# Random tie-breaking, with one seed, in the list scheduler of a fused attention and channel-mix kernel

## The chip, the cores and the metric

The kernel runs on one core of a Trainium2 chip. The metric is the device time of one execution in microseconds (us). It holds the whole computation, from the inputs in HBM to the output in HBM. The core's engines are named as the profile names them: PE (TensorE, matmuls) with PEld (its weight loads), DVE (VectorE), ACT (ScalarE), POOL (GpSimd) and SP (SyncE, which here only issues DMAs).

## The reference

Softmax attention with RMS-normalised queries and keys over batch 8, 12 heads, 448 tokens, head size 64. Its output, as 768 features per token, goes through a channel mix: each token is blended with the one before it by two learned vectors, multiplied by `w_k` (768 x 1024), clipped at zero and squared, multiplied by `w_v` (1024 x 768), and gated by the sigmoid of a second blend times `w_r` (768 x 768). Everything is float32 at the surface; the three weight matrices come in float64.

```python
q_n, k_n = rmsnorm(q, g_q), rmsnorm(k, g_k)
scores = scale * np.matmul(q_n, k_n.transpose(0, 1, 3, 2))
attn = np.exp(scores - np.max(scores, axis=-1, keepdims=True))
attn = attn / (np.sum(attn, axis=-1, keepdims=True) + 1e-09)
attn_out = np.matmul(attn, v)
...
xk = mu_k * x + (1.0 - mu_k) * x_prev
xr = mu_r * x + (1.0 - mu_r) * x_prev
k = np.maximum(xk @ w_k, 0.0)
v = k * k @ w_v
r = 1.0 / (1.0 + np.exp(-(xr @ w_r)))
return (r * v).astype(np.float32)
```

## The kernel before

**Tiling.** The work on the attention side goes by quads of heads (24 of them, `quads`) and pairs (48, `pairs`). A quad has seven score groups, each a tile of 128 rows by 448 keys for two heads. Most products are formed from two 16-bit parts of each operand, high and low, so that a product is three matmuls; the first three quads (`U32 = 3`) use 32-bit matmuls instead. After each pair's attention, two blends of the token with its predecessor are made (`mix`), and when the six pairs of a batch are there, the MoE part of the batch follows: eight 448-wide products with `w_k` (`moe`, `square`), then for each block of 128 tokens and each half of the features a product with `w_r` and one with `w_v` (`gate`, `store`). The weights are decoded from float64 and split into 16-bit parts in the course of the first quarter of the run (`wload`, `weights`, `wsplit`).

**Who does what.** PE does all matmuls and, for the early groups, transposes. DVE finds the row maxima of scores (`expo`), forms low parts (`split`), blends, decodes weights and multiplies by the gate. ACT does exponentials, high parts, casts and activations. POOL does scalings and differences in SBUF. SP issues the loads of q, k and v, the DMA transposes of probabilities and of q and k, and the stores; ACT issues the weight loads.

**Buffers.** PSUM has eight banks in one ring, of which scores may hold five (`SC_SHARE`), the MoE products and the weight decoding two (`MM_SHARE`), and attention outputs and weight statistics two (`OT_SHARE`). There are three q/k buffers, two V buffers, four tiles for probabilities (`NAT_BUFS`, one more later).

**What sets the order.** The order of instructions on each engine is not written out; a planner, `Plan`, makes it while the program is built. Every piece of work (`load`, `stats`, `preps`, `expo`, `split`, `weights`, `moe` and so on) is a Python generator, called a thread, that yields one operation after another, or a condition to wait for. The planner keeps one clock per engine, in nanoseconds, from a price list (`price` for DVE, ACT and POOL; the matmuls' price stands in their `form`; DMAs are priced in `emit`). `advance` fetches a thread's next operation and works out when its operands are ready by the planner's own account. `run` then takes, over and over, the operation with the smallest key:

```python
k = max(self.clk[th[2][0].eng] + wait, th[3] + slack) - PS * (th[1]() if callable(th[1]) else th[1])
if best is None or k < key:
    best, key = th, k
```

Here `th[3]` is the readiness, `th[1]` the thread's priority and `PS` is 0.1, so that a hundred points of priority are worth 10 ns. `slack` holds matmuls of attention back (`MARGIN` 600, `MARGIN_A` 400, `MARGIN_V` 1200), `wait` charges a switch of the PE tile mode (`SWITCH` 600) and one kind of ACT sequence (`ACC_GAP` 130). The comparison is strict, so of equal keys the one whose thread stands first in the list of threads wins: the thread that was spawned earlier. Priorities that matter for ties are `PRIO_E` 400 (`expo`, `probs`, `setup`, `load`), `PRIO_M` 400 (`square`, `gate`, `store`), `PRIO_R` 320, `PRIO_V` 310, `PRIO_O` 300, `PRIO_P` 200 (`split`), `PRIO_S` 150 (`scores`), `PRIO_Q` and `PRIO_A` 50 (`stats`, `preps`, `attends`), 0 (`mixk`, `moe`), and for the weights one formula that all their threads share (`wprio`). `pick` chooses ACT or DVE for some copies out of PSUM (in `turn` and `probs_pe`, for the first three quads) by whose clock is behind.

The planner prices TensorE at one speed throughout. All instructions are recorded by one helper line, so the profile shows L273 for nearly all of them; they are told apart by their tiles. `ps` is a PSUM bank, `sums` the maxima and sums of a score group, `nat` a tile of probabilities or of prepared q and k, `stk` transposed q and k, `pT` transposed probabilities, `wf` a decoded weight block, `raw` its float64 words, `kk` the squared activations, `xk` and `xr` the two blends. In the first stretch, buffers of `kk` and `xk` are lent out for other tiles (`KK_LENT`, `XK_LENT`), so that these two names then also stand for raw weights, loaded q and k, or probabilities.

Of the kernel before, what the change touches and what calls it, by code (L numbers as in the profile page):

```python
# [1 line left out]

# [52 lines left out]
PS = 0.1  # L55
# [75 lines left out]
class Op:  # L131
    def __init__(self, eng, fn, kw, form=None):
        self.eng, self.fn, self.kw, self.form = eng, fn, kw, form
        outs = [kw[k] for k in ("out", "accum_out") if kw.get(k) is not None]
        self.reads = [span(x) for k, x in kw.items() if k not in ("out", "accum_out") and hasattr(x, "tensor")]
        self.writes = [span(x) for x in outs if hasattr(x, "tensor")]
        self.reads = [y for x in self.reads for y in x]
        self.writes = [y for x in self.writes for y in x]
# [64 lines left out]
        return lambda form=None, **kw: Op(self.name, f, {k: aps(x) if hasattr(x, "shape") else x for k, x in kw.items()}, form)  # L203


class Plan:
    LAT = 35

    def __init__(self, tc):
        self.tc = tc  # L210
        self.clk = dict.fromkeys(("PE", "DVE", "ACT", "POOL", "SP"), 0.0)
        self.last, self.use, self.threads = {}, {}, []
        self.form, self.dma_free, self.acc, self.n = None, {"SP": 0.0, "ACT": 0.0}, False, 0
        self.held = {"DVE": [], "POOL": []}

    def margin(self, form):
        if form == "moe":
            return 0
        if form == "av" and self.st["want"] != "xk":
            return MARGIN_A  # L220
        return MARGIN_V if form == "v" else MARGIN
# [5 lines left out]
        return min(self.clk["ACT"], self.clk["DVE"])  # L227

    def spawn(self, gen, prio=0):
        th = [gen, prio, None, 0.0]  # L230
        self.threads.append(th)
        self.advance(th)

# [13 lines left out]
    def advance(self, th):  # L247
        try:
            x = next(th[0])
        except StopIteration:  # L250
            self.threads.remove(th)
            return
        if isinstance(x, Op):
            x = [x]
        th[2] = x
        th[3] = self.ready(x) if isinstance(x, list) else 0.0

    def note(self, op, fin):
# [66 lines left out]
    def run(self):  # L325
        while self.threads:
            best, key = None, None
            for th in list(self.threads):
                if not isinstance(th[2], list):
                    if not th[2]():  # L330
                        continue
                    self.advance(th)
                    if th not in self.threads or not isinstance(th[2], list):
                        continue
                slack = self.margin(th[2][0].form[0]) if th[2][0].eng == "PE" else 0
                mode = MODE.get(th[2][0].form[0], 0) if th[2][0].eng == "PE" else None
                wait = SWITCH if mode == 0 and self.form else 0
                if self.acc and th[2][0].eng == "ACT" and th[2][0].kw.get("accum_out") is not None:
                    wait += ACC_GAP
                k = max(self.clk[th[2][0].eng] + wait, th[3] + slack) - PS * (th[1]() if callable(th[1]) else th[1])  # L340
                if best is None or k < key:
                    best, key = th, k
            if best is None:
                if any(isinstance(th[2], list) or th[2]() for th in self.threads):
                    continue
                assert not self.threads, [(th[0].__name__, th[2]) for th in self.threads]
                break
            r = self.ready(best[2])
            if r > best[3] + 1:
                best[3] = r  # L350
                continue
            self.emit(best[2])
            self.advance(best)
# [884 lines left out]
```

## Time and profile before

| | |
|---|---|
| median of 3 runs | 1015.41 us (1015.3 to 1017.15) |
| the profiled execution's own time | 1015.21 us |
| its span, first to last instruction | 1013.4 us |
| PE busy | 926.0 us, 91% of the span |
| DVE busy | 812.7 us, 80% |
| ACT busy | 746.0 us, 74% |
| POOL busy | 691.8 us, 68% |
| mean granted TensorE clock | 0.961 |
| bytes moved | 148.17 MB, 146 GB/s |

The busy times are of the whole span; the engines do different work early and late, so the stretches have to be read one by one. A busy PE is not a PE at its peak, since its matmuls overlap. A row of waits gives the engine and tile that stood idle, the engine and tile that ended the idle time, the total, the number of waits and the longest. A timeline row gives the start, the length, the engine, and the operation with output and inputs; in brackets stand the idle time of the engine ahead of it and what ended it.

### The profile page before, as it was taken

The page shows a single profiled execution, that of the slowest core. Times are in us where ns is not written, and L with a number is a line of the kernel's source. Part 1 is how long each engine was busy: PE and PEld are TensorE (multiplying, and loading weights), DVE is VectorE, ACT ScalarE, POOL GpSimd, SP SyncE. Part 2 cuts the span into 40 slices and gives each one's busy share as a digit, 9 for nine tenths or more (in the row PEclk, how much of TensorE's full clock was granted, in tenths as well). Part 3 has the DMA queues.
Part 4 walks back from the last instruction along what each step waited for, and adds up shares of the span by engine and source line. Part 5 has one row for each costly group of instructions (what it writes and reads, how often), then busy time and mean ns, then how long its engine had stood idle before and what let it go on. Part 6 is the DMA issues. An engine that isn't in the chain of part 4 may idle for free. (4 is left out here: it accounts for less than half of the span.)

```text
span 1013.4 us, 18593 instructions
## 1 busy us (share of the span) xinstructions
PE 926.0 (91%) x6082; PEld 485.8 (48%) x6082; DVE 812.7 (80%) x2260; ACT 746.0 (74%) x1756; POOL 691.8 (68%) x734
## 2 busy tenths in 40 slices
PE   2588869669999999999999999899999999999998
PEld 2354434335544555455545555355545454455564
DVE  5879998999998698979997998799997989763000
ACT  3667878878788789888887887878886988952311
POOL 2787889743798747877886859855987478556501
PEclk9878979869999999999999999999999999999999
DMA  7322349667788789569847977869858884640000
GB/s 248 119 80 86 118 120 221 170 166 169 172 165 168 143 197 203 133 152 201 207 105 173 214 158 161 161 131 201 175 126 177 186 183 110 146 107 32 1 32 32
DMA packets 371138, 148.17 MB, mean 146 GB/s; under 512 B 338272, under 2 KB 355168, under 8 KB 371040
## 3 DMA queue, kind: packets, MB, share of 16 engines
q1 hardware_dynamic: 351792, 129.20, 57.0%
q10 hardware_dynamic: 19248, 17.77, 5.9%
q8 instruction: 48, 0.79, 0.3%
q14 instruction: 50, 0.41, 0.1%
HBM read 51.98 MB, written 11.01 MB: 62 GB/s over the span
## 5 line engine op out<-in xcount | busy, mean ns | idle before, releaser
L273 PE MATMUL ps<-wvh,kk 128*128 128x384 f16 x896 | 233.1, 326 | 0.8 <-DVE nat L273 0.8
L273 ACT ACTIVATE ps<-ps,sums 128x448 f32<-128x448 f32 x294 | 181.9, 621 | 52.5 <-DVE sums L273 48.9
L273 PE MATMUL ps<-xk,wkh 128*128 128x448 f16 x768 | 210.5, 356 | 4.8 <-DVE wf L273 3.9
L273 DVE SCALAR_TENSOR_TENSOR nat<-ps,sums,nat 128x64 f16<-128x64 f32 x480 | 190.7, 439 | 19.2 <-ACT nat L273 17.8
L273 DVE TENSOR_REDUCE sums<-ps 128x1 f32<-128x448 f32 x336 | 193.7, 612 | 15.4 <-PE ps L273 15.1
L273 PE MATMUL ps<-wrh,xr 128*128 128x384 f16 x672 | 179.9, 331 | 2.1 <-DVE nat L273 2.0
L273 ACT ACTIVATE nat<-ps,sums 128x448 f16<-128x448 f32 (+1 forms) x272 | 167.8, 659 | 16.9 <-DVE sums L273 7.1
L273 PEld LDWEIGHTS <-kk 128*128 128x128 f16 (+1 forms) x1362 | 129.2, 98 | 98.7 <-issue 13.5
L273 PE MATMUL ps<-stk 64*128 64x448 f16 (+3 forms) x1104 | 134.2, 390 | 26.4 <-ACT xk L273 6.2
L273 PE MATMUL ps<-wvl,kk 128*128 128x384 f16 x448 | 146.0, 326 | 0.0
L273 PE MATMUL ps<-xk,wkl 128*128 128x448 f16 x384 | 136.5, 355 | 0.0
L273 PEld LDWEIGHTS <-xr 128*128 128x128 f16 x1008 | 96.4, 99 | 80.1 <-issue 16.9
L273 PE MATMUL ps<-wrl,xr 128*128 128x384 f16 x336 | 111.1, 331 | 0.0
L273 PEld LDWEIGHTS <-wkh 128*128 128x128 f16 x768 | 71.9, 99 | 81.6 <-issue 21.6
L273 POOL TENSOR_TENSOR o<-o,bsc 128x384 f32<-128x384 f32 x48 | 43.3, 902 | 88.3 <-DVE o L273 52.3
L273 DVE SCALAR_TENSOR_TENSOR o<-o,ps 128x384 f32<-128x384 f32 x56 | 30.5, 545 | 87.7 <-PE ps L273 59.2
L273 PE MATMUL ps<-pT,vh 128*64 128x448 f16 x588 | 93.8, 363 | 1.4 <-DMA pT<-nat 0.7
L273 ACT ACTIVATE o<-ps,bsc 128x128 f32<-128x128 f32 x144 | 45.6, 387 | 51.2 <-PE ps L273 33.1
L273 POOL TENSOR_TENSOR qk<-qk,ss 128x896 f32<-128x896 f32 x36 | 64.0, 1778 | 22.1 <-DVE ss L273 14.9
L273 PEld LDWEIGHTS <-stk 64*128 64x128 f16 x1008 | 35.0, 98 | 78.0 <-issue 35.5
L273 DVE SCALAR_TENSOR_TENSOR df<-x,bsc,df 128x448 f32<-128x448 f32 x68 | 61.0, 910 | 5.8 <-POOL df L273 5.7
L273 POOL TENSOR_TENSOR nat<-nat 128x448 f32<-128x448 f32 x41 | 48.2, 1175 | 23.6 <-ACT nat L273 17.1
(161 smaller groups left out, 1813.7 us busy)
## 6 DMA issues: line engine op xcount, KB each, us to landing
vf<-in_v_dram SPq DMA_DIRECT2D x48, 256.0 KB, 3.0
out_dram<-o SPq DMA_DIRECT2D x28, 384.0 KB, 2.7
qk<-in_k_dram SPq DMA_DIRECT2D x23, 448.0 KB, 4.4
qk<-in_q_dram SPq DMA_DIRECT2D x22, 448.0 KB, 4.3
raw<-in_moe_w_v_dram ACTq DMA_DIRECT2D x12, 512.0 KB, 4.2
raw<-in_moe_w_r_dram ACTq DMA_DIRECT2D x12, 384.0 KB, 3.3
kk<-in_moe_w_k_dram ACTq DMA_DIRECT2D x8, 384.0 KB, 3.9
raw<-in_moe_w_k_dram ACTq DMA_DIRECT2D x8, 384.0 KB, 3.7
```

Source lines behind the costliest of these rows:

```text
L273: r = op.fn(op.kw["out"], op.kw["value"]) if op.fn.__name__ == "memset" else op.fn(**op.kw)
```

## The change

A fifth field is added to each thread: a random number between 0 and `AMP` = 10 (nanoseconds), drawn anew whenever `advance` has fetched the thread's next operation or condition, and kept until the next. `run` adds it to the key. The generator is Python's, seeded with `SEEDS[g]`; with one seed in the list and a segment length of a second, `g` is always 0 and the one stream starts from seed 415. The seed is one that gives a short schedule on the planner's own clocks. Nothing else in the planner, the prices or the kernel is touched.

```diff
+from random import Random
...
+SEEDS = [415]
+AMP = 10.0
+SEG = 1e9
...
+        self.seg = -1
+
+    def noise(self):
+        g = min(len(SEEDS) - 1, int(min(self.clk.values()) / SEG))
+        if g != self.seg:
+            self.seg, self.rng = g, Random(SEEDS[g])
+        return AMP * self.rng.random() if SEEDS[g] else 0.0
...
-        th = [gen, prio, None, 0.0]
+        th = [gen, prio, None, 0.0, 0.0]
...
         th[2] = x
+        th[4] = self.noise()
         th[3] = self.ready(x) if isinstance(x, list) else 0.0
...
-                k = max(self.clk[th[2][0].eng] + wait, th[3] + slack) - PS * (th[1]() if callable(th[1]) else th[1])
+                k = max(self.clk[th[2][0].eng] + wait, th[3] + slack) - PS * (th[1]() if callable(th[1]) else th[1]) + th[4]
```

## The prediction

> **What bounds the kernel now.** I read the page first: busy time by engine, then the 40 slices.
>
> ```profile
> span 1013.4 us, 18593 instructions
> PE 926.0 (91%) x6082; PEld 485.8 (48%) x6082; DVE 812.7 (80%) x2260; ACT 746.0 (74%) x1756; POOL 691.8 (68%) x734
> PE   2588869669999999999999999899999999999998
> PEclk9878979869999999999999999999999999999999
> ```
>
> The slices say that this is not one regime but two. In the first ten slices (some 253 us) TensorE has holes and its granted clock is below full; from there on it is nearly solid at full clock. So I asked for the busy time in three stretches, and in two short ones inside the first.
>
> ```profile
> 0.00:253.00 253.00, 185.50 (x1106) 100.66 (x1107) 218.75 (x622) 183.50 (x412) 174.63 (x206) 0.86 0.56 149
> 253.00:912.00 659.00, 643.84 (x4408) 329.46 (x4406) 580.28 (x1619) 541.00 (x1293) 481.19 (x490) 0.99 0.75 164
> 912.00:1013.40 101.40, 96.63 (x572) 55.68 (x569) 13.62 (x20) 21.48 (x52) 36.02 (x39) 1.00 0.06 24
> 130.00:140.00 10.00, 3.58 (x26) 1.53 (x26) 10.00 (x28) 7.68 (x19) 9.59 (x14) 0.66 0.54 151
> 140.00:150.00 10.00, 8.67 (x35) 3.99 (x35) 9.29 (x25) 6.13 (x14) 8.50 (x9) 0.66 0.35 105
> ```
>
> Columns are the stretch, its length, then busy PE, PE weight load, DVE, ACT and POOL, and the granted clock. TensorE is idle 253 - 185.5 = 67.5 us in the first stretch, 15.2 us in the second and 4.8 us in the last, the drain. DVE, by contrast, is busy 218.75 of the first 253 us: the start is bound by DVE and by what waits in its queue, the rest by TensorE. The chain of waits says the same from the end:
>
> ```profile
> 873.69 128.13 PE ps L273 x805
> ```
>
> From 873.69 on TensorE runs 805 matmuls without a break, and nothing else decides. An order that the planner changes can therefore only pay through a TensorE wait before 873.69 us that gets shorter, or through matmuls that no longer run at a lowered clock; each microsecond so won ahead of the wall moves the wall by one microsecond. So I list TensorE's waits, first those before 253 us, then those from 253 to 912 us (total us, number, longest).
>
> ```profile
> PE ps L273 <- DVE nat L273: 22.4, 5, 18.7
> PE ps L273 <- DVE wf L273: 12.3, 9, 3.9
> PE ps L273 <- ACT xk L273: 6.2, 1, 6.2
> ...
> PE ps L273 <- DVE mucol L273: 0.2, 1, 0.2
> ```
>
> ```profile
> PE ps L273 <- DMA stk<-natx: 5.7, 2, 3.8
> ...
> PE ps L273 <- DMA pT<-nat: 0.7, 1, 0.7
> ...
> PE ps L273 <- ACT vh L273: 0.5, 2, 0.3
> ```
>
> The first list has 18 rows and 43 waits in all. The longest, 18.7 us, is the start, before any operand exists. That leaves 42 waits and 67.5 - 18.7 = 48.8 us, 1.2 us each. The second list has 7 rows, 17 waits and 15 us.
>
> **The change, part by part.** *Instructions.* The random number is drawn while the program is written; it adds no instruction and takes none away. The one place where the instruction mix can move is the choice between ACT and DVE for copies out of PSUM in the first three head quads, which asks whose clock is behind:
>
> ```profile
> L273 DVE COPY pT<-ps 128x512 f32<-128x512 f32 x8 | 5.4, 683 | 0.6 <-PE ps L273 0.6
> ```
>
> ```profile
> L273 ACT COPY pT<-ps 128x512 f32<-128x512 f32 x13 | 7.5, 587 | 1.7 <-PE ps L273 1.7
> ```
>
> Both rows are from the groups of the first 253 us by form (count, then total us and mean ns). Three copies that change sides shift 3 x 0.68 = 2 us of DVE work onto ACT, or back; of either sign, and DVE's idle time in that stretch covers it in part. I take it at nothing, bounds -2 to +2 us.
>
> *What the noise can reorder.* A thread's key is the later of its engine's clock and its operands' readiness, minus 0.1 x its priority, plus now a draw from 0 to 10 ns held until the operation is issued. Two operations whose keys are d ns apart swap with probability (10 - d)^2 / 200: one in two for exact ties, 0.13 at 5 ns, under 0.01 at 9 ns, none past 10 ns. Exact ties are common: on a backlogged engine every ready operation has the engine's clock as its time, and equal priorities are many (400 for score reductions, exponentials, MoE evacuations and transposes of probabilities; one common value for all weight steps; 50 for statistics, preparation and attend where no boost is on). They used to go to the oldest thread; now it is a lottery, so an older operation can be passed. TensorE's own margins (400 to 1200 ns) and the 600 ns against switching tile modes are out of reach of 10 ns: its sequence moves only because operands come earlier or later.
>
> *What one swap costs.* It moves an operation by one instruction of the same engine, on DVE most often by one of these:
>
> ```profile
> L273 DVE TENSOR_REDUCE sums<-ps 128x1 f32<-128x448 f32 x84 | 49.0, 613 | 9.6 <-PE ps L273 9.4
> L273 DVE SCALAR_TENSOR_TENSOR nat<-ps,sums,nat 128x384 f16<-128x384 f32 x37 | 22.3, 603 | 0.0
> ```
>
> that is 0.61 us. A look at the longest wait of the weight group shows how such a step reaches TensorE:
>
> ```profile
> 139.19 0.52 ACT L273 ACTIVATE ps<-raw 128x384 f32<-128x384 f32 x1
> ...
> 139.68 0.61 DVE L273 TENSOR_REDUCE sums<-ps 128x1 f32<-128x448 f32 x1
> ...
> 140.41 0.55 DVE L273 SCALAR_TENSOR_TENSOR wf<-ps,raw 128x384 int32<-128x384 int32 x1
> ...
> 141.01 0.53 PE L273 MATMUL ps<-xk,wkh 128*128 128x448 f16 x1 [3.90 <-DVE wf L273]
> ```
>
> ACT fills the MoE bank by 139.71, DVE runs a reduction of another group first, the weight step ends at 140.96, and only then does TensorE get the bank, after 3.9 us of idling. Had the weight step gone ahead, TensorE would have started about 0.6 us sooner; with one more reduction in front, 0.6 us later.
>
> *The sum.* I cannot follow which of the 42 + 17 = 59 waits gets which sign, so I treat them as 59 independent steps of 0.61 us either way: a redrawn order then spreads the end by 0.61 x sqrt(59) = 4.7 us (an estimate from these rows). Blind, its mean would be zero. But the seed is taken for a short plan, and a plan that is short has the good signs at TensorE as the planner sees them. How far do its clocks hold? It prices a 448-wide reduction from PSUM at 448/0.96 + 144 = 611 ns, the row says 613; a chunk of six 448-wide matmuls at 1135 ns, and at full clock two halves of a chunk start 0.56 us apart (rows under B), so 1.12 us. Engine by engine it holds; it has no lowered TensorE clock, and a DMA lands after a fixed time. Between no carry-over (0 us) and two spreads (9.4 us) I take one, 4.7 us, because the costs are near but the waits it models are of the same size as what it leaves out. For the profiled execution: 1013.4 - 4.7 = 1008.7 us of span; its own time was 1015.21 us (1.8 us around the span) and the median of the runs is 1015.41, so I subtract from the median: 1010.7 us.
>
> *Queues.* Loads, V loads, DMA transposes and stores share SP's queue, and loads tie exactly with the transposes of probabilities at 400. SP stands most of its time at the head of that queue for a producer:
>
> ```profile
> SPq L273 <- DVE nat L273: 200.3, 74, 14.1
> ```
>
> A load put behind a waiting transpose waits with it, up to 14.1 us in one case. The cover is the buffering (three q/k buffers, two V buffers): TensorE waited for transposes only 5.7 + 0.7 us in the second stretch, so I cost swaps on SP at nothing, and at up to 3.8 us, the longest of those waits, where the cover is gone. For MoE evacuations the cover is the other bank: while one of the two is emptied, TensorE runs 18 matmuls or more into the other, nearly 3 us at 0.16 us each by the wall's 128.13 us / 805; two or three lost ties on DVE in a row stay hidden.
>
> **The rivals.** *A: the noise mostly swaps equals (no change).* The commonest exact ties are twins: the two halves of a score group, the two split steps. Swapping twins changes nothing, since their consumer waits for both. For it: 643.84 of 659 us solid TensorE, and this stretch is most of the span. Against: one flip changes the clocks that every later choice is made on. Time 1015.4, give or take 2.0.
>
> *B: more clock loss (slower).* The two short stretches above show the clock at 0.66 around the 3.9 us wait, and the matmuls after it are slow:
>
> ```profile
> 141.71 0.58 PE L273 MATMUL ps<-xk,wkl 128*128 128x448 f16 x1
> ...
> 147.05 0.35 PE L273 MATMUL ps<-xk,wkl 128*128 128x448 f16 x1
> ```
>
> ```profile
> 160.28 0.35 PE L273 MATMUL ps<-xk,wkl 128*128 128x448 f16 x1
> ...
> 160.84 0.35 PE L273 MATMUL ps<-xk,wkl 128*128 128x448 f16 x1
> ```
>
> These are the last matmuls of triples. From 141.71 to 147.05 five triples took 5.34 us, 1.07 us each, where at full clock one takes 0.56 us and five take 2.80. One more such wait in the first stretch costs 3.9 + 2.5 = 6.4 us: 1021.8 us. The planner prices a chunk alike in both states, so a seed may look short and still buy this. It decides from the point where a tie leaves TensorE without work for about the 3.6 to 3.9 us seen here, and where the waits before 253 us grow past 48.8 us. The Trainium skill's page TensorE: Matmul & The Clock Gate (Part 1) states the rule behind it: the array runs at half rate until a window of about 3.4 us was busy, and falls back after an idle one. By that rule, the trace agrees: 1.07 against 0.56 us per triple.
>
> *C: a large gain.* DVE's idle time bounds the first stretch: 253 - 218.75 = 34.3 us, of which 7.8 us lie in the first 10:
>
> ```profile
> 0.00:10.00 10.00, 0.00 (x0) 0.00 (x0) 2.22 (x11) 2.64 (x4) 1.82 (x7) 1.00 0.56 194
> ```
>
> If the seed closes half of the other 26.5 us, TensorE's wall starts 13.2 us sooner: 1002.2 us. For it: DVE would then be busy 218.75 of 239.8 us, 91%, hardly more than the 88% (580.28 of 659 us) that it holds through the second stretch. Against: 13.2 us is nearly three of the spreads above.
>
> **How the numbers follow.** A measurement of this kernel tells about 0.2% (2.0 us) from no change. Forecast, a gain of 2 to 9 us: 0.38. C, over 9 us: 0.10. A: 0.22. B, at its full price or a part of it: 0.30, since a redraw has both signs and the planner is blind to the clock. Faster is 0.38 + 0.10 = 0.48, same 0.22, slower 0.30. The forecast's own range is 1006 to 1013.4. The range for 8 in 10 reaches to most of B and of C: 1002 to 1022, leaving about 0.06 below and 0.12 above.
>
> **What would show it.** Right: the same number of instructions to within some ten copies; TensorE idle time before 253 us below 67.5 by a few microseconds, in the rows wf, nat and xk; the last wall of matmuls as long as before, about 128 us or a little more, starting some 5 us earlier; matmuls of the wall still 0.16 us apart. A is right if both lists of waits change their members but not their sums. B is right if the clock of the first stretch falls below 0.86 and a wait of over 3.6 us is added. C is right if TensorE turns solid by some 240 us, with DVE over 90% busy up to there. The forecast is wrong altogether if TensorE is starved after 253 us by more than the 15 us of now, for then the swaps reach the wall through buffers that I took as cover.

## The result, and the profile after

| | before | after |
|---|---|---|
| median | 1015.76 us (4 runs, 1015.3 to 1017.15) | 1023.65 us (4 runs, 1022.15 to 1024.38) |
| ratio, 95% interval | | 1.0073 [1.0056, 1.0091] |
| the profiled execution's own time | 1015.21 us | 1022.15 us |
| its span | 1013.4 us | 1020.1 us |
| mean granted TensorE clock | 0.961 | 0.968 |
| end on the planner's own clocks | 977.9 us | 970.2 us |

The change makes the kernel 7.9 us slower. The last row is what the scheduler believed: its clocks, read off when the program had been written, say 7.6 us shorter. So the seed does what the change says, and the chip answers with the opposite sign. First the page of the kernel after, the head and TensorE's slices, to be held against the lines of before in the prediction (after has 14 lines more, so the helper's line is L287 here):

```profile
span 1020.1 us, 18522 instructions
PE 919.6 (90%) x6082; PEld 486.9 (48%) x6082; DVE 810.6 (79%) x2262; ACT 749.2 (73%) x1754; POOL 689.0 (68%) x734
PE   2688879559998999999999999999999999999998
PEclk9798989769999999999999999999999999999999
```

The work is the same: two copies changed from ACT to DVE, and the other engines' counts are equal (the 71 instructions that the total has fewer are not counted as an engine's work). TensorE is even 6.4 us less busy, 5.0 of them in the first stretch, where its mean granted clock is 0.87 instead of 0.86. Busy time per stretch of the kernel after (stretch, length, then busy PE, PE weight load, DVE, ACT and POOL, granted clock, DMA share, GB/s):

```profile
0.00:253.00 253.00, 180.53 (x1106) 99.89 (x1107) 219.34 (x631) 184.25 (x413) 175.90 (x211) 0.87 0.59 150
253.00:912.00 659.00, 635.67 (x4359) 327.56 (x4357) 574.10 (x1609) 539.90 (x1282) 470.71 (x476) 1.00 0.76 162
912.00:1020.00 108.00, 103.36 (x621) 59.40 (x618) 17.11 (x24) 25.04 (x60) 42.35 (x49) 1.00 0.10 31
```

TensorE's idle time is 72.5 us in the first stretch (67.5 before), 659 - 635.67 = 23.3 us in the second (15.2 before), and 1020.1 - 919.6 = 100.5 us in all against 87.4. That is 13.1 us more idling, 6.4 us less busy time, and so 6.7 us more span. The first stretch does the same number of matmuls in both (1106): its 5.0 us of shorter busy time and its 5.0 us of longer idling cancel. What is new is the dense stretch, where DVE too does less: 574.10 us of work in the same 659 us, against 580.28.

The chain of waits after, its last wall in four pieces, and the page's shares by engine:

```profile
872.36 13.87 PE ps L287 x95
886.27 5.11 PE ps L287 x40
891.41 16.93 PE ps L287 x115
908.36 100.19 PE ps L287 x608
```

```profile
PE 15%; DVE 8%; ACT 3%; POOL 3%; issue 2%; DMA 0%; POOLq 0%; DVEq 0%; ACTq 0%
```

Before, the page's line read:

```profile
PE 19%; DVE 1%; POOL 1%; issue 1%; DMA 1%; ACT 0%; POOLq 0%; DVEq 0%; ACTq 0%
```

The four pieces follow one another within 0.05 us, so they are one wall: 858 matmuls in 136.2 us, 0.16 us each as before. TensorE's pace is unchanged; but at 872 us it still has 858 matmuls to do, where before it had 805 at 873.69, and 53 of 0.16 us are 8.5 us. And the chain ahead of the wall has hardly any matmuls: as far back as its pieces are listed, from 715 to 872 us, it runs through DVE, ACT and POOL, that is through softmax, preparation of q and k and the blends, apart from 12.9 us of TensorE (89 matmuls at 765 us). Before, the listed chain began at 775 us and held 62.6 us of TensorE. This does not mean that TensorE stands still there: it is busy 153.1 of these 157 us (154.2 before). Of the 53 matmuls that are late, 49 are lost earlier, from 253 to 715 us, where TensorE does 3040 instead of 3089.

TensorE's waits from 250 to 860 us, before and then after (total us, number, longest; the rows left out are below 1 us each, ACT x with 1.1 us apart):

```profile
PE ps L273 <- DVE natx L273: 3.8, 4, 1.8
PE ps L273 <- DMA stk<-natx: 3.8, 1, 3.8
PE ps L273 <- DVE nat L273: 2.9, 5, 0.8
```

```profile
PE ps L287 <- DVE nat L287: 6.6, 8, 1.6
PE ps L287 <- DVE natx L287: 4.8, 7, 1.3
PE ps L287 <- ACT vh L287: 3.5, 3, 1.7
PE ps L287 <- DVE sums L287: 1.3, 1, 1.3
PE ps L287 <- DVE vs L287: 1.3, 1, 1.3
```

All rows together come to 13.1 us in 16 waits before and 21.9 us in 29 after. `nat` and `natx` are the probabilities that DVE's split step makes out of a score bank; when they are late, so is the bank. And what DVE and ACT wait for in the same stretch, on the path of those banks:

```profile
DVE sums L273 <- ACT ps L273: 8.2, 14, 1.2
```

```profile
DVE sums L287 <- ACT ps L287: 22.0, 35, 1.8
```

```profile
ACT ps L273 <- DVE sums L273: 39.0, 37, 5.4
```

```profile
ACT ps L287 <- DVE sums L287: 56.7, 58, 3.1
```

The first pair: DVE waits for the sums that come with ACT's exponentials. The second: ACT waits for DVE's maxima. The first has more than doubled, the second has grown by 45%. The two engines hand a score group back and forth (maxima on DVE, exponentials on ACT, reciprocal and split on DVE), and after the change each waits more often for the other.

### The profile page after: what moved, and what is told of

It is laid out like the page before. It is cut to its first block, busy times and chain, and to the rows that moved or that the text cites. A ratio compares the mean times of both kernels' runs of the same rounds, so it can differ in the third digit from the quotient of the medians.

```text
span 1020.1 us, 18522 instructions
## 1 busy us (share of the span) xinstructions
PE 919.6 (90%) x6082; PEld 486.9 (48%) x6082; DVE 810.6 (79%) x2262; ACT 749.2 (73%) x1754; POOL 689.0 (68%) x734
## 5 line engine op out<-in xcount | busy, mean ns | idle before, releaser
L287 ACT ACTIVATE ps<-ps,sums 128x448 f32<-128x448 f32 x294 | 179.6, 614 | 81.3 <-DVE sums L287 69.1
L287 PE MATMUL ps<-wvh,kk 128*128 128x384 f16 x896 | 234.4, 327 | 2.0 <-DVE sums L287 1.3
L287 PE MATMUL ps<-xk,wkh 128*128 128x448 f16 x768 | 210.0, 355 | 3.6 <-POOL xk L287 1.2
L287 DVE SCALAR_TENSOR_TENSOR nat<-ps,sums,nat 128x64 f16<-128x64 f32 (+1 forms) x488 | 194.6, 441 | 20.2 <-ACT nat L287 19.8
L287 DVE TENSOR_REDUCE sums<-ps 128x1 f32<-128x448 f32 x336 | 194.3, 614 | 18.6 <-PE ps L287 14.1
L287 ACT ACTIVATE nat<-ps,sums 128x448 f16<-128x448 f32 (+1 forms) x280 | 170.9, 650 | 26.6 <-DVE sums L287 21.7
L287 PEld LDWEIGHTS <-kk 128*128 128x128 f16 (+1 forms) x1362 | 128.4, 98 | 113.4 <-issue 16.9
L287 PE MATMUL ps<-wrh,xr 128*128 128x384 f16 x672 | 176.0, 326 | 2.3 <-DVE nat L287 2.3
L287 PE MATMUL ps<-stk 64*128 64x448 f16 (+3 forms) x1104 | 129.8, 382 | 18.9 <-DVE nat L287 5.1
L287 PE MATMUL ps<-wvl,kk 128*128 128x384 f16 x448 | 146.0, 326 | 0.0
L287 PE MATMUL ps<-xk,wkl 128*128 128x448 f16 x384 | 136.0, 354 | 0.0
L287 PEld LDWEIGHTS <-xr 128*128 128x128 f16 x1008 | 96.4, 98 | 71.7 <-issue 6.6
L287 PE MATMUL ps<-wrl,xr 128*128 128x384 f16 x336 | 109.5, 326 | 0.0
L287 PEld LDWEIGHTS <-wkh 128*128 128x128 f16 x768 | 71.8, 98 | 79.0 <-issue 16.8
L287 POOL TENSOR_TENSOR qk<-qk,ss 128x896 f32<-128x896 f32 x36 | 63.5, 1764 | 55.1 <-DVE ss L287 37.6
L287 DVE SCALAR_TENSOR_TENSOR o<-o,ps 128x384 f32<-128x384 f32 x56 | 30.5, 545 | 85.4 <-PE ps L287 57.0
L287 PE MATMUL ps<-pT,vh 128*64 128x448 f16 x588 | 94.5, 364 | 2.1 <-DVE natx L287 0.7
L287 POOL TENSOR_TENSOR o<-o,bsc 128x384 f32<-128x384 f32 x48 | 42.9, 893 | 68.0 <-DVE o L287 43.0
L287 ACT ACTIVATE o<-ps,bsc 128x128 f32<-128x128 f32 x144 | 43.9, 384 | 45.3 <-PE ps L287 32.1
L287 PEld LDWEIGHTS <-stk 64*128 64x128 f16 x1008 | 35.6, 98 | 77.9 <-issue 36.9
L287 POOL TENSOR_TENSOR nat<-qk,nat 128x896 f16<-128x896 f32 x31 | 59.0, 1903 | 16.4 <-ACT nat L287 16.4
L287 DVE SCALAR_TENSOR_TENSOR df<-x,bsc,df 128x448 f32<-128x448 f32 x68 | 66.7, 986 | 3.3 <-POOL df L287 3.1
```

The lines of the kernel that those rows point to most:

```text
L287: r = op.fn(op.kw["out"], op.kw["value"]) if op.fn.__name__ == "memset" else op.fn(**op.kw)
```

## The experiments

The theories, in words. *Lot* (L and R in the expectations): drawing ties by a random number is itself a worse rule than the oldest first, and the chip pays for it where the planner's clocks see nothing. *Seed* (T in some of the expectations): the rule is neutral, and this seed is an unlucky one; the chip adds its own scatter to any plan. *Fortunate* (D): any redraw of the order does worse than before, because before was a lucky order, of which nothing tells but its time. *Price* (P): a wrong price in the planner makes it pick orders that are bad on the chip. Theory N says that differences of this size between plans do not reach the chip; S and W, in the later expectations, say which threads' ties matter. The expectations below stand as they were written, misses included.

For each kernel I also read the planner's end off its clocks. The difference between the chip's median and that end is the kernel's *offset*: what the chip adds to the plan. Before has 37.9 us, after 53.4 us. The table holds all of them, in the order of the text.

| kernel | ties | planned end | chip, us (runs) | ratio to before, 95% | offset | DVE sums <- ACT ps, 250 to 860 us |
|---|---|---|---|---|---|---|
| before | oldest | 977.9 | 1015.8 | | 37.9 | 8.2 us, 14 |
| after | lot | 970.2 | 1023.65 (4) | 1.0073 [1.0056, 1.0091] | 53.4 | 22.0, 35 |
| seed101 | lot | 966.6 | 1014.9 (8) | 0.9989 [0.9972, 1.0006] | 48.3 | 17.0, 37 |
| seed123 | lot | 971.0 | 1027.02 (2) | 1.0118 [1.0072, 1.0163] | 56.0 | 10.6, 23 |
| seed17 | lot | 977.9 | 1033.0 (2) | 1.0176 [1.0134, 1.0219] | 55.1 | 15.1, 31 |
| seed126 | lot | 992.6 | 1051.78 (2) | 1.0361 [1.0315, 1.0408] | 59.2 | 16.1, 33 |
| ties9 | lot, exact ties only | 978.7 | 1031.81 (2) | 1.0163 [1.0085, 1.0241] | 53.1 | 17.3, 31 |
| youngest | youngest | 984.5 | 1045.85 (2) | 1.0301 [1.0243, 1.0359] | 61.4 | 24.6, 56 |
| old_lat34 | oldest | 980.2 | 1017.69 (8) | 1.0016 [1.0004, 1.0029] | 37.5 | 9.7, 12 |
| old_op9995 | oldest | 971.9 | 1022.94 (4) | 1.0061 [1.002, 1.0101] | 51.0 | 11.2, 15 |
| late_only | oldest, then lot | 977.1 | 1026.56 (2) | 1.0112 [1.0082, 1.0142] | 49.5 | 22.8, 40 |
| early_only | lot, then oldest | 978.7 | 1022.73 (2) | 1.0074 [1.0051, 1.0097] | 44.0 | 9.1, 18 |
| fix_old | oldest, price mended | 974.9 | 1013.84 (10) | 0.9982 [0.9959, 1.0004] | 38.9 | 11.1, 15 |
| fix_seed16 | lot, price mended | 975.9 | 1025.07 (2) | 1.0097 [1.0075, 1.012] | 49.1 | 15.0, 29 |
| soft54 | lot in softmax only | 977.4 | 1035.34 (2) | 1.0196 [1.0128, 1.0264] | 57.9 | 13.6, 30 |
| soft18 | lot in softmax only | 977.5 | 1024.39 (4) | 1.0091 [1.0046, 1.0135] | 46.9 | 19.6, 39 |
| other7 | lot outside softmax | 977.3 | 1025.91 (2) | 1.0103 [1.0036, 1.017] | 48.6 | 13.5, 18 |
| other13 | lot outside softmax | 977.3 | 1018.84 (8) | 1.0035 [1.0015, 1.0055] | 41.5 | 11.5, 17 |
| best94 | lot outside softmax, price mended | 970.9 | 1013.14 (12) | 0.9977 [0.9963, 0.9991] | 42.2 | 8.1, 13 |
| best167 | lot outside softmax | 970.4 | 1010.01 (5) | 0.9953 [0.9936, 0.997] | 39.6 | 9.9, 14 |

### Other seeds: does the plan say anything?

Four seeds of different planned length, nothing else changed (101, 126, 17, 123):

```diff
-SEEDS = [415]
+SEEDS = [101]
```

> Seed 101 instead of 415, nothing else. On the planner's own clocks this plan ends at 966.6 us, the unseeded one at 977.9, seed 415 at 970.2. Theory T (the clocks carry over, seed 415 was merely unlucky on the chip): 1012 us, 11 below the middle of the seeds (plan plus 45.6 us, the mean of 37.9 for the unseeded order and 53.4 for seed 415). Theory N (differences between plans of this size do not reach the chip): 1020 us give or take 5, like any other seed.

> Seed 126, the longest plan of the 160 looked at: 992.6 us on the planner's clocks. Theory T: 1038 us (plan plus 45.6). Theory N: 1020 us give or take 5; in between if a part carries over.

> Seed 17, whose plan ends at 977.9 us, exactly as long as the unseeded one. Theory T: the time of the unseeded order, 1015.8 us, or at most 1023.5 by the mean offset. A third theory, L (the old rule, the oldest thread first, is itself worth something on the chip that the clocks do not show): 1023 us, some 7 slower than the unseeded order at the same planned length.

> Seed 123, planned end 971.0 us, nearly that of seed 415. Theory T: 1016.6 us by the mean offset. Theory N: 1020 give or take 5. Theory L: 1023 to 1025, as for seed 415.

With after, five seeds planned at 966.6, 970.2, 971.0, 977.9 and 992.6 us took 1014.9, 1023.65, 1027.02, 1033.0 and 1051.78 us: the same order. From the shortest to the longest the plan grows by 26.0 us and the chip by 36.9. So among lots the planner's ranking carries over in full, and a search over seeds does find better ones. But the line lies too high: seed17 has the planned end of before to a tenth and takes 1.0176 [1.0134, 1.0219] of its time. The offsets of the five are 48 to 59 us. An unlucky seed 415 is thereby out as the whole cause; a shift that all lots share is left.

Where that shift arises can be dated. The planner's clock at the end of every MoE chunk stands against the same chunk's last matmul in the trace. At a planned time of 240 us the chip is behind by 20.1 us in before, 20.6 in after, 16 to 24 in the other seeds; from there to the end the lag grows by 13.1 us in before, 26.9 in after and 26 to 35 in the other four. The loss is in the dense stretch.

### Exact ties alone, the youngest first, and other orders under the old rule

Is it the noise of up to 10 ns, which passes operations that are not tied, or the exact ties?

```diff
-SEEDS = [415]
-AMP = 10.0
+SEEDS = [9]
+AMP = 1e-6
```

> The changed kernel with AMP at 1e-6 ns and seed 9: only exact ties are drawn by lot, no difference of priority is overridden. Planned end 978.7 us. Theory R: 1033 us (offset 54), since exact ties alone undo the rule; if it is the overriding of small priorities that hurts, 1017 us. Theory D: 1033 us too.

And the opposite of the old rule, without any lot (one character in the kernel before), so that of equal keys the thread spawned last wins:

```diff
-                if best is None or k < key:
+                if best is None or k <= key:
```

> The kernel before with the comparison not strict, so that of equal keys the thread that stands last in the list wins: the youngest first, and no random number. Planned end 984.5 us. Theory R: the suspected cost at its fullest, an offset of 54 or more, 1038 to 1050 us. Theory D: offset 54, 1038 us.

ties9 has an offset of 53.1 us, like after: exact ties are enough. youngest (one order) has 61.4 us, the largest of all, and its TensorE waits from 250 to 860 us come to 32.7 us. The offset follows the age rule, 38 for the oldest, about 53 for a lot, 61 for the youngest. That is what *lot* needs and what *seed* has no reason for.

Against *fortunate* I redrew the order under the old rule, by shaking one constant of the planner so little that only the choices change:

```diff
-    LAT = 35
+    LAT = 34
```

> The kernel before, oldest thread first, no noise, with the planner's signal latency LAT at 34 instead of 35 ns: the order is redrawn and the rule is kept. Planned end 980.2 us (977.9 with 35). Chip time minus planned end was 37.9 us for the unseeded order and 48 to 59 us for the five seeded ones. Theory R (the rule that the oldest goes first is what the chip rewards): offset near 38, so 1018 us. Theory D (the unseeded order was one fortunate draw, and any redraw loses it): offset near 54, so 1034 us.

```diff
-OP_SLOW = 1.0
+OP_SLOW = 0.9995
```

> The kernel before, no noise, with the prices of DVE, ACT and POOL multiplied by 0.9995: a second redraw that keeps the rule. Planned end 971.9 us, as short as a good seed. Theory R: 1010 us, faster than before. Theory D: 1026 us.

old_lat34 has before's offset (37.5). old_op9995 does not: 51.0, as if it had been a lot. Its plan was the shorter by 6.0 us, and it lost them and 7 more on the chip. One redraw for *lot*, one for *fortunate*; the second I could not explain, and it stays an exception.

### Which half of the program

The seed's two halves, with the switch at a planned 240 us. In late_only the first 240 us are those of before to the instruction, and lots are drawn afterwards, by a stream of seed 415 that starts there; early_only is the reverse.

```diff
-SEEDS = [415]
+SEEDS = [0, 415]
...
-SEG = 1e9
+SEG = 240e3
```

> Noise only once the slowest of the planner's clocks is past 240 us (SEEDS [0, 415], SEG 240e3): the first stretch is the unseeded order to the letter, the lot decides in the dense stretch only. Planned end 977.1 us. So far chip minus plan was 38 us for two orders that keep the rule, 51 for a third, and 48 to 61 for the seven that break ties otherwise; the difference arose after 240 us. Theory R (lots in the dense stretch let the chip fall behind the plan): 1028 to 1033 us. If the damage is done in the first stretch: 1015 us.

```diff
-SEEDS = [415]
+SEEDS = [415, 0]
...
-SEG = 1e9
+SEG = 240e3
```

> The reverse (SEEDS [415, 0]): the first 240 us are those of the changed kernel, then the oldest thread goes first again. Planned end 978.7 us. Theory R: offset 38, 1017 us. Theory D (the unseeded order was one fortunate draw): offset 54, 1033 us. If the loss sits in the first stretch: above 1025 us.

late_only keeps the loss, 1.0112 [1.0082, 1.0142] at a planned end 0.8 us shorter than before's. Its DVE wait for the exponentials in the dense stretch, against that of early_only:

```profile
DVE sums L287 <- ACT ps L287: 22.8, 40, 1.9
```

```profile
DVE sums L287 <- ACT ps L287: 9.1, 18, 1.7
```

The fingerprint goes with the half in which lots are drawn. early_only's offset, 44.0, lies between those of before and after, though. Dated as above, it is behind by 22.3 us at a planned 240 us and loses 17.7 more, against 20.1 and 13.1 in before: most of the difference arises in the half where no lots are drawn, and why was not found.

### The price of a short step

The planner prices the 64-wide split step at 64/0.96 + 64 = 131 ns, because its rule for two PSUM-sided operands says `n > 64`. In the traces such steps follow one another every 192 ns, and the mean of one, in the groups of before by form, is this (count, total us, mean ns):

```profile
L273 DVE SCALAR_TENSOR_TENSOR nat<-ps,sums,nat 128x64 f16<-128x64 f32 x240 | 65.8, 274 | 19.2 <-ACT nat L273 17.8 <-POOL natx L273 1.1
```

The Trainium skill's page Perfetto Trace Analysis, section Optimizing Scalar/DVE Operations, gives about 125 ns of access overhead for DVE on PSUM. With the price list's 64/0.96 for the elements that makes 192 ns, an estimate, and the trace agrees for this step. So 294 steps (240 and 54 of `natx`) are 61 ns too cheap, 18 us of DVE in all. *Price* says that this draws the planner into orders that are late on the chip.

```diff
-        c = n / 0.96 + (128 if two and n > 64 else 64)
+        c = n / 0.96 + (128 if two and n >= 64 else 64)
```

> The kernel before, no noise, with one price mended: a two-input DVE step 64 wide is priced at 195 ns instead of 131 (n >= 64 in place of n > 64), as the traces have it, 192 ns from start to start. Planned end 974.9 us. Theory P (the plans' blindness to this step, 240 of them in the dense stretch, some 61 ns each, is a main part of what the chip loses against the plan): offset 28 to 33, 1003 to 1008 us, faster than both kernels. If the price does not matter: offset 38, 1013 us; theory D: 1029 us.

> The changed kernel with the same price mended and seed 16, the shortest of 160 under the mended price: planned end 975.9 us. Theory P: the offset of seeded orders falls from 53 to about 43, 1019 us. If the price does not matter: 1029 us.

fix_seed16 has the same edit in the kernel after, with seed 16. The offsets hardly move: 38.9 with the oldest first, 49.1 by lot. The gap between the rules is there with the right price as well, so on these two orders the price is not its cause. fix_old itself measures 0.9982 [0.9959, 1.0004], which can't be told from no change.

### Which ties

The softmax chain of a score group are the threads `expo`, `probs` and `split`. First lots only there, two seeds (54 and 18) of a planned length close to before's:

```diff
-        th[4] = self.noise()
+        th[4] = self.noise() if th[0].__name__ in ("expo", "probs", "split") else 0.0
```

> Noise only for the threads of the softmax chain (expo, probs, split), seed 54; all others keep the oldest-first rule. Planned end 977.4 us (unseeded 977.9). Theory S (it is the order of score groups in the softmax chain that the chip minds): offset 53, 1030 us. Theory W (it is the other threads' ties): offset 38 to 44, 1018 us. If both count: 1025 us.

> As soft54 with seed 18, planned end 977.5 us. Theory S: 1030 us. Theory W: 1018 us. Both: 1025 us.

Then lots everywhere but there, seeds 7 and 13, again near before's length:

```diff
-        th[4] = self.noise()
+        th[4] = 0.0 if th[0].__name__ in ("expo", "probs", "split") else self.noise()
```

> The reverse: noise for every thread but those of the softmax chain, seed 7. Planned end 977.3 us. Theory S: offset 38 to 44, 1018 us. Theory W: offset 53, 1030 us. Both: 1025 us.

> As other7 with seed 13, planned end 977.3 us. Theory S: 1018 us. Theory W: 1030 us. Both: 1025 us.

All four plans end at 977.3 to 977.5 us. Lots in the chain give offsets of 57.9 and 46.9 us, lots elsewhere 48.6 and 41.5: in the mean 52.4 against 45.1. The waits of DVE for the exponentials separate without overlap, 30 and 39 against 18 and 17. The times don't: other7 is no faster than soft18. Two seeds of each are too few to price the chain alone; the kernels of the next section add two more with lots outside it.

### Lots where they do no harm, and a short plan

If the chain keeps the oldest first, a short plan should keep its gain on the chip. best94 has the edit above, the mended price and seed 94; best167 the edit alone and seed 167, which was the shortest of 200 plans.

```diff
-SEEDS = [415]
+SEEDS = [167]
...
-        th[4] = self.noise()
+        th[4] = 0.0 if th[0].__name__ in ("expo", "probs", "split") else self.noise()
```

> Oldest first in the softmax chain, lots elsewhere, 64-wide DVE step priced at 195 ns, seed 94, the shortest of 240 plans: planned end 970.9 us. If the seed's gain carries over where the chain keeps its rule: the offset of fix_old, 39 us, or a few more, so 1010 to 1013 us, faster than both kernels. If lots cost the chip the same wherever they are drawn: offset 49 as for fix_seed16, 1020 us.

> As best94 with the price left as it was, seed 167, the shortest of 200 plans: planned end 970.4 us, as short as the changed kernel's 970.2. If the chain's rule is the main part: offset 45 (mean of other7 and other13), 1015 us, 8 below the changed kernel. If lots cost the same wherever they are drawn: offset 53, 1023 us.

Both are slightly faster than before: 0.9977 [0.9963, 0.9991] and 0.9953 [0.9936, 0.997]. best167 has after's planned end (970.4 against 970.2 us) and takes 13.6 us less on the chip. The pair speaks for *lot*: plans of one length, with and without lots in the chain. The seeds differ too (415 and 167), so it is one order of each kind; the weight lies on the groups of orders below. Busy time per stretch, for after and for best167:

```profile
250.00:860.00 610.00, 587.34 (x4032) 302.98 (x4031) 532.93 (x1488) 499.75 (x1184) 445.62 (x449) 1.00 0.77 164
```

```profile
250.00:860.00 610.00, 597.85 (x4098) 307.51 (x4096) 552.41 (x1527) 508.57 (x1210) 459.28 (x460) 1.00 0.77 167
```

In the same 610 us TensorE gets 66 more matmuls done (66 of 0.16 us are 10.6 us), DVE 39 and ACT 26 more instructions. The waits of best167 that answer to those of after:

```profile
PE ps L287 <- DVE nat L287: 4.9, 8, 1.0
...
PE ps L287 <- DVE natx L287: 0.5, 1, 0.5
```

```profile
DVE sums L287 <- ACT ps L287: 9.9, 14, 1.5
```

```profile
ACT ps L287 <- DVE sums L287: 37.6, 30, 3.6
```

The two probability rows of TensorE together, DVE's waits and ACT's are back near where they were before the change (6.7, 8.2 and 39.0 us).

### How an order reaches TensorE

One wait of the kernel after in close-up: DVE's rows (start, length, operation, in brackets the idle time ahead and its releaser), then TensorE's.

```profile
428.84 0.79 DVE L287 SCALAR_TENSOR_TENSOR nat<-ps,sums,nat 128x64 f16<-128x64 f32 x2
430.08 0.28 DVE L287 SCALAR_TENSOR_TENSOR natx<-ps,sums,natx 128x64 f16<-128x64 f32 x1 [0.45 <-ACT natx L287]
430.28 1.15 DVE L287 TENSOR_REDUCE sums<-ps 128x1 f32<-128x448 f32 x2
431.34 1.33 DVE L287 SCALAR_TENSOR_TENSOR natx<-ps,sums,natx 128x64 f16<-128x64 f32 x3
```

```profile
432.20 0.74 PE L287 MATMUL ps<-stk 64*128 64x448 f16 x6 [1.28 <-DVE natx L287]
```

DVE has begun the split of one group (430.08), then takes the two maxima of another (430.28 to 431.34), and only then goes on with the first. The score matmuls that need the first group's bank stand still for 1.28 us: 1.06 of it are the two maxima, and 0.19 the short step of the group's other half. TensorE did nothing else in that time; its order is fixed when the program is written.

This place shows how DVE's order reaches TensorE. It does not show a lot that put the maxima there: `expo` has priority 400 and `split` 200, so their keys lie 20 ns apart when both are ready, as they are in the planner at this step, and a draw of up to 10 ns can't turn that. What ties here are the split steps of the group's two halves, and that is the 0.19 us. Over the stretch, TensorE idles ahead of the 16-bit score matmuls for 9.9 us from 250 to 860 us before, 14.4 after and 7.6 in best167 (groups by form).

Which ties the lot turned can be read off the planner of the kernel after, from a planned 240 to 870 us. On DVE it passed over the older of two tied split steps or maxima 105 times within one score group (its two halves) and 105 times between two groups. Ties between split steps of two groups stand at the head of DVE's choices 95 times there, and 38 times in the planner of before: with lots, two groups are in work side by side more often.

### What holds, and what stays open

Over all kernels, eight orders that keep the oldest first in the softmax chain throughout (before, old_lat34, old_op9995, fix_old, other7, other13, best94, best167) have a mean offset of 42.1 us with a standard deviation of 5; ten that draw lots in it (after, the four seeds, ties9, soft54, soft18, fix_seed16, late_only) have 52.9 with 4. The waits of DVE for ACT's exponentials number 12 to 18 in the first group and early_only, 23 to 56 in the second and youngest.

The mean planned ends of the two groups are near each other, 975.1 and 976.5 us, so it is not that one group has the more hopeful plans. So it is shown that a lot in the chain, in the dense stretch, goes with more ping-pong between DVE and ACT and, in the mean, with some 11 us more than the plan says, and that the mean follows the rule, though single orders of the two groups overlap. Parted further, the mean offset is 41.3 us with the oldest first everywhere (4 orders), 43.0 with lots outside the chain alone (4), 52.4 with lots in the chain alone (2) and 53.5 with lots everywhere from the start (7): nearly all of the difference goes with the chain. (late_only, with lots in the dense stretch only, has 49.5.) Plans don't show it: on the planner's clocks TensorE idles 2.5 us between 220 and 870 us in after and 8.6 in before, against 23.3 and 15.2 on the chip from 253 to 912.

Why the chip minds is not shown. My reading is that a chain in which two groups alternate has each hand-over on its path, so that every small excess over the priced latency is paid at once, where the oldest-first order has other work between; that reading was argued, not isolated. Swaps within a group and swaps between groups were not run apart either.

Open are the 51.0 us of old_op9995 and the 48.6 of other7, which have the old rule in the chain, few waits for the exponentials, and an offset like a lot; the number of these waits marks the rule, it does not price it (seed123 has 23 of them and 56.0 us). Whatever else spreads the offsets by some 5 us I could not find. Lots in the chain alone were run with two seeds only, so the chain's share of the 11 us is known by the means alone.

## Why the prediction was wrong

It forecast 1010.7 us; 1023.65 us lies above its range, which ended at 1022. Point by point:

- **Two regimes, and a wall of TensorE at the end.** Right for before. After it is no longer so: the wall begins at about the same time and paces alike, but holds 53 matmuls more, because less had been done by then.
- **The instruction mix.** Right: two copies changed sides, 0 to 2 us were allowed.
- **The size of a redraw.** 59 waits of 0.61 us gave a spread of 4.7 us. On the planner's clocks 160 seeds spread by 4.5 us (standard deviation; mean 980.5, 966.6 to 992.6). That the two numbers are near may be luck: the 59 waits are counted on the chip, the spread of the seeds on the planner's clocks. On the chip five seeds, the shortest and the longest plan among them, are spread further, 36.9 us for 26.0.
- **"Blind, its mean would be zero."** This is the step that failed. The working took a redrawn order as 59 steps of either sign around the old one. But the old order is not one draw among many: it is made by a rule, the oldest thread first, and orders drawn by lot lie some 11 us above it on the chip (52.9 against 42.1 us of offset), and 2.6 us above it on the planner's clocks (980.5 against 977.9). By these figures a blind lot ends near 980.5 + 52.9 = 1033.4 us, an estimate: the term that was put at nothing is about 17.6 us, and the seed's short plan brought about 9.8 us of it back. I had written down that equal keys "used to go to the oldest thread; now it is a lottery", and gave that no price.
- **The carry-over of the planned gain.** "Engine by engine it holds" was right among lots: the ranking of five seeds carried over, and the planned 7.6 us were worth about what they promised against another lot (seed17, planned 7.7 us longer, took 9.4 us longer). Against the oldest first, the 7.6 us of plan are used up by the 15.5 us of offset (53.4 - 37.9): the sum is the 7.9 us that were measured. The gain was to come out of the waits ahead of 253 us, which were to fall below 67.5 us; they came to 72.5.
- **The cover.** I looked for cover in SP's queue and in the two MoE banks, and there it held: TensorE's waits for DMA in the dense stretch fell to 0.6 us. The longer waits are those for the score groups' banks, which I did not look at. The prediction's own last sentence named this outcome: "if TensorE is starved after 253 us by more than the 15 us of now". It is starved by 23.3 us.
- **Rival A, equals swapped.** No: ties9, with exact ties alone, has an offset of 53.1 us. Its premise was that the commonest ties are twins, whose consumer waits for both. Half of the chain's ties that the lot turned on DVE were not twins (105 of 210), and twins are not quite equals: each half of a group gives its bank back by itself at the end of its own `split`, so the order of the steps sets when a bank comes free.
- **Rival B, more clock loss.** Its sign was right and its mechanism wrong: the clock of the first stretch is 0.87 against 0.86, of the whole 0.968 against 0.961. The waits of that stretch did grow, as the rival asked: TensorE's first matmul came at 12.1 us instead of 18.7, and the waits behind it make 72.5 - 12.1 = 60.4 us instead of 48.8. But four of them are over 3.6 us, as many as before, the clock did not fall, and the shorter busy time of the stretch paid for its 5.0 us of idling.
- **Rival C.** No: the first stretch did not close up. What best167 gained lies in the dense stretch.

## What to carry to other kernels

The tie rule of a list scheduler is a policy: here lots in a chain of hand-overs between two engines went with some 11 us on the chip that the planner's clocks don't show, against the oldest first. Search over seeds only among orders made by one rule, compare the offset between chip and plan before trusting a shorter plan, and date that offset by stage. Leave the chain that frees the bottleneck's buffers out of the lottery: here two orders of the same planned length, with lots in the chain and without, took 1.0073 and 0.9953 of the time before.

## What the runs showed of the hardware

A DVE step with one operand in PSUM and one in SBUF costs some 125 ns beside its elements, narrow or wide, if the elements are counted as the price list has them: 64 wide it takes 192 ns from start to start (64/0.96 = 67), 384 wide 525 ns (384/0.96 = 400). A 448-wide reduction out of PSUM, with one operand, takes 531 ns from start to start, that is 64 ns beside its 467. These are medians of the trace of before; the mean lengths of one instruction, 274, 605 and 612 ns, are longer, since the next one starts before the last has ended.

On ACT, two exponentials with accumulation in direct succession start 0.705 us apart, and 0.57 to 0.58 us where another operation follows the first (medians of before and after). This does not part the orders: of direct successions that start within 0.76 us, before has 70, after 93 and best167 93 too.

Two steps changed their lengths between the kernels without being touched, the 448-wide `df` and `dfx` steps of DVE on SBUF, in opposite ways, by the groups of before and of after (count, total us, mean ns):

```profile
L273 DVE SCALAR_TENSOR_TENSOR df<-x,bsc,df 128x448 f32<-128x448 f32 x68 | 61.0, 910 | 5.8 <-POOL df L273 5.7
L273 DVE SCALAR_TENSOR_TENSOR dfx<-x,bsc,dfx 128x448 f32<-128x448 f32 x28 | 31.6, 1130 | 4.1 <-POOL dfx L273 4.1
```

```profile
L287 DVE SCALAR_TENSOR_TENSOR df<-x,bsc,df 128x448 f32<-128x448 f32 x68 | 66.7, 986 | 3.3 <-POOL df L287 3.1
L287 DVE SCALAR_TENSOR_TENSOR dfx<-x,bsc,dfx 128x448 f32<-128x448 f32 x28 | 26.6, 949 | 2.2 <-POOL dfx L287 2.2
```

Together they take 92.6 us before and 93.3 after, and 97.1 in best167, the fastest kernel. So their length does not go with the offset. What lies beside such a step, POOL's work on SBUF among it, differs with the order; whether that is what changes its length was not tested.
